# Linear attention and a GELU MLP in one kernel: a written-out order for the first group's attention, and idle matmuls between the first transposes

## The chip, the cores and the metric

The kernel runs on one core of a Trainium2 chip. The metric is the device time of one execution in microseconds (us), lower is better. TensorE (PE) multiplies matrices, VectorE (DVE), ScalarE (ACT) and GpSimd (POOL) work elementwise, SyncE (SP) issues transfers; GpSimd issues transfers too, and each such issue takes its time.

## The reference

Linear attention with a decay per head, then a two-layer MLP. Batch 4, 8 heads, 768 positions, head size 64; 3072 tokens of width 512, hidden width 2048. Inputs and output are float32.

```python
for b in range(nb):                       # blocks of 64 positions
    intra = einsum('bhic,bhjc->bhij', qb, kb) * Dmask      # Dmask = lam**(i-j), i >= j
    intra = einsum('bhij,bhjd->bhid', intra, vb)
    inter = einsum('bhid,bhde->bhie', qb * lam_pow, kv_state)
    out[:, :, sl] = intra + inter
    kb_dec = kb * rev_pow                                  # lam**(63-pos)
    kv_state = lam_block * kv_state + einsum('bhsd,bhse->bhde', kb_dec, vb)
x = out.transpose(0, 2, 1, 3).reshape(3072, 512)
h = x @ w_in
y = (0.5 * h * (1 + erf(h / sqrt(2)))) @ w_out
```

## The kernel before

The attention goes by chunks of 128 positions, all heads at once: 24 chunks, six for each batch entry. For a chunk the steps are: load k, q and v (cast to bf16 on the way, issued by GpSimd); k^T and q^T with the decay in them (`transposes` on TensorE, or `dma_transposes` by SyncE, for which GpSimd first makes q_hat); `scores` = k^T q^T, masked into sc_m by VectorE; `decay_k`, k times its decay; `next_state`, which adds k_dec^T v to the state (kv_ps); `outputs`, state times q^T plus v times sc_m, emptied into x_t, the transposed input of the MLP.

The MLP goes by groups of four chunks (512 tokens), six groups. A group has 32 blocks of 4 matmuls: 16 blocks of the first layer (`mm1`: h_ps, then GELU on ScalarE into g_t), and 16 of the second (`mm2`: o_ps, then ScalarE copies to o_sb and SyncE writes it out). In group 0 the second layer goes through outputs 0 and 1 in turn, then 2 and 3 in turn.

The chunks 0 to 3 are the opening (`early`), written out by hand with idle matmuls (`keep_warm`) between. The attention of a later chunk n is put among the MLP's blocks of the group before its own: chunks 4 to 7 in group 0, 8 to 11 in group 1, and so on. A table of fractions (`fs`) sets before which block the four steps of a chunk stand: begin (decay on GpSimd, and the loads of a chunk some steps ahead, `prefetch`), transposes, scores with the next state, and outputs. Chunks 4 to 7 use TensorE's transposes, later ones the transposing DMA.

The program is a manual schedule: each engine executes its instructions in the order in which the code emits them, and waits at each for what it needs. So a load that GpSimd issues can stand behind a decay that waits for data, and the other way round. In the order lists and traces, L65 is a load, L87 and L91 the weights' loads, L167 a decay of k on GpSimd, L178 a transpose, L200 scores, L237 a state, L252 and L262 the two parts of outputs, L268 the copy into x_t, L280 and L292 the MLP's matmuls.

The PSUM banks limit what can be in flight: two for "mh" (h_ps, and k^T in the opening), two for "mo" (the second layer, idle matmuls, and q^T in the opening), two for scores, one "t" (transposes of chunks 4 to 7, and kv_ps), one "o" (outputs of the attention).

Of the kernel before, what the change touches and what calls it, by code (L numbers as in the profile page):

```python
# [8 lines left out]
F32 = mybir.dt.float32  # L9
BF16 = mybir.dt.bfloat16  # L10
# [5 lines left out]
def kernel(  # L16
# [10 lines left out]
    nc = tc.nc  # L27
# [11 lines left out]

    M = 4  # L40
    NG = NCH // M
    assert NG * M == NCH and M < NB

    ctx.enter_context(tc.manual_schedule())

# [17 lines left out]
    def load(n, name):  # L63
        raw[n, name] = qkv_pool.tile([128, H, D], BF16, tag=name, name=f"{name}_t")
        nc.gpsimd.dma_start(raw[n, name], chunk_of(name, n))  # L65
# [82 lines left out]
    def bank(shape, dtype, tag, name):  # L148
        return ps.tile(shape, dtype, tag=tag, name=name, bufs=2 if tag in ("sc", "mh", "mo") else 1)
# [7 lines left out]
    def decay_k(c, eng):  # L157

        if c.sb == NB - 1:
            return  # L160
        c.k_dec = work_pool.tile([128, H, D], BF16, tag="kd", name="k_dec")
        if eng is nc.scalar:
            for h in range(H):
                nc.scalar.activation(c.k_dec[:, h, :], c.k[:, h, :], ACT.Copy, scale=lam_k[:, h:h + 1])
        else:
            scale = lam_k if c.early else lam_m
            eng.tensor_mul(c.k_dec, c.k, scale[:, :, None].to_broadcast((128, H, D)))  # L167

    def transposes(c):
        if c.early:  # L170

            t_ps = [bank([128, HP, C], BF16, tag, "t_ps") for tag in ("mh", "mo")]
        else:
            both = bank([128, 2, HP, C], BF16, "t", "t_ps")
            t_ps = [both[:, 0], both[:, 1]]
        for dst, src in zip(t_ps, (c.k, c.q)):
            for hp in range(HP):
                nc.tensor.transpose(dst[:, hp, :], src[:, 2 * hp:2 * hp + 2, :], ident)  # L178
        c.kT = work_pool.tile([128, HP, C], BF16, tag="kT", name="kT")
        c.qT = work_pool.tile([128, HP, C], BF16, tag="qT", name="qT")  # L180
        if c.early and c.n % 2:
            nc.scalar.copy(c.kT, t_ps[0])
        else:
            nc.vector.tensor_copy(c.kT, t_ps[0])  # L184
        nc.vector.tensor_mul(c.qT, t_ps[1], lam_q)  # L185
# [20 lines left out]
    def next_state(c):  # L206
        if c.sb == NB - 1:
            return
        if not c.early:
            return next_state_full(c)  # L210
        kv_ps = bank([128, HP, D], F32, "t", "kv_ps")
        for hp in range(HP):
            for hi in range(2):
                h = 2 * hp + hi
                nc.tensor.matmul(kv_ps[hi * D:(hi + 1) * D, hp, :], c.k_dec[:, h, :], c.v[:, h, :],
                                 start=True, stop=True)
# [11 lines left out]
        old = work_pool.tile([128, HP, D], F32, tag="old", name="old")  # L228
        for hp in range(HP):
            nc.scalar.activation(old[:, hp, :], new[:, hp, :], ACT.Copy, scale=lam_c[:, hp:hp + 1])  # L230
        states[c.n + 1] = new, old

    def next_state_full(c):

# [10 lines left out]
            nc.vector.tensor_mul(new, tmp, lam_blk)  # L245
        states[c.n + 1] = new, None

    def outputs(c, x_t, off):
        o_ps = bank([128, HP, C], F32, "o", "o_ps")
        if c.sb > 0 and not c.early:  # L250
            for hp in range(HP):
                nc.tensor.matmul(o_ps[:, hp, :], states[c.n][0][:, hp, :], c.qT[:, hp, :],  # L252
                                 start=(hp == 0), stop=False, skip_group_check=True)
        elif c.sb > 0:
            for hp in range(HP):
                for hi in range(2):
                    p = slice(hi * D, (hi + 1) * D)
                    nc.tensor.matmul(o_ps[p, hp, :], states[c.n][0][p, hp, :], c.qT[p, hp, :],
                                     start=(hp == 0), stop=False, skip_group_check=True)
        for hp in range(HP):  # L260
            for hi in range(2):
                nc.tensor.matmul(o_ps[hi * D:(hi + 1) * D, hp, :], c.v[:, 2 * hp + hi, :], c.sc_m[:, hp, hi, :],  # L262
                                 start=(c.sb == 0 and hp == 0), stop=True, skip_group_check=True)
        x_o = x_t[:, :, off * C:(off + 1) * C]
        if c.early:
            nc.scalar.copy(x_o, o_ps)
        else:
            nc.vector.tensor_copy(x_o, o_ps)  # L268


    def mlp_blocks(g):
# [4 lines left out]
        def mm1(kf):  # L276
            def run():
                h_ps = bank([128, T], F32, "mh", "h_ps")
                for ki in range(NK1):
                    nc.tensor.matmul(h_ps, w_in_t[:, ki, kf * 128:(kf + 1) * 128], x_t[:, ki, :],  # L280
                                     start=(ki == 0), stop=(ki == NK1 - 1))
# [61 lines left out]
    make_dmask()  # L343
    nc.scalar.activation(warm, pos, ACT.Gelu)

    def keep_warm(n):

        idle_ps = bank([128, 512], F32, "mo", "idle_ps")
        for _ in range(n):
            nc.tensor.matmul(idle_ps, idle[:, :128], idle, start=True, stop=True)  # L350

    def early(s):
        live[s] = begin(s, early=True)
        transposes(live[s])
        decay_k(live[s], nc.scalar if s < 2 else nc.gpsimd)
# [9 lines left out]
    outputs(live[0], xT[0], 0)  # L365
    scores(live[1])
    load_w_in(0)
    keep_warm(1)
    early(2)
    next_state(live[1])  # L370
    scores(live[2])
    outputs(live[1], xT[0], 1)
    keep_warm(1)
    early(3)
    next_state(live[2])
# [12 lines left out]

    total = NK2 * 4 * M * C + M * NK2 * 512
    todo = []  # L390
    for n in range(M, NCH):
        g, i = n // M - 1, n % M
        if g == 0:
            fs = [0.66 + 0.34 * (i + f) / M for f in (-0.5, 0.0, 0.5, 1.05)]
        else:
            at = 0.04 + 0.25 * i
            fs = [at - (0.15 if n == 2 * M else 0.32), None, at, at + 0.25 if i < M - 1 else 0.965]
        todo += [(round((g + f) * total), -kind, n) for kind, f in enumerate(fs) if f is not None]
    todo.sort()
# [61 lines left out]
```

## Time and profile before

| | |
|---|---|
| median of 9 runs | 223.72 us (223.31 to 226.08) |
| profiled execution | 223.31 us, span 221.5 us |
| PE busy | 207.3 us, 94% of the span |
| DVE, ACT, POOL busy | 77.2, 87.6, 104.9 us |
| DMA | 24.35 MB, mean 110 GB/s |
| chain that ended last | PE 77%, DMA 10%, POOL 9% of the span |

A row of the timeline reads: start in us, duration in us, engine, source line, operation, output tile <- input tiles, shape, count, and in brackets the idle time ahead of it with the releaser. A row of the waits reads: total us, times, longest us. "PEclk" is the clock granted to TensorE, as a share of full speed. The landing of a transfer is counted from its issue.

### The profile page before, as it was taken

The page shows a single profiled execution, that of the slowest core. Times are in us where ns is not written, and L with a number is a line of the kernel's source. Part 1 is how long each engine was busy: PE and PEld are TensorE (multiplying, and loading weights), DVE is VectorE, ACT ScalarE, POOL GpSimd, SP SyncE. Part 2 cuts the span into 40 slices and gives each one's busy share as a digit, 9 for nine tenths or more (in the row PEclk, how much of TensorE's full clock was granted, in tenths as well). Part 3 has the DMA queues.
Part 4 walks back from the last instruction along what each step waited for, and adds up shares of the span by engine and source line. Part 5 has one row for each costly group of instructions (what it writes and reads, how often), then busy time and mean ns, then how long its engine had stood idle before and what let it go on. Part 6 is the DMA issues. An engine that isn't in the chain of part 4 may idle for free.

```text
span 221.5 us, 3569 instructions
## 1 busy us (share of the span) xinstructions
PE 207.3 (94%) x1423; PEld 103.8 (47%) x1447; DVE 77.2 (35%) x128; ACT 87.6 (40%) x168; POOL 104.9 (47%) x120
## 2 busy tenths in 40 slices
PE   7789999499799999999999999999999999999993
PEld 2454444255445454444455444544445544444452
DVE  4795000458841362133264243035235233100000
ACT  6985671110255611265511365412365321467121
POOL 8998333899999999084981535032100000000000
PEclk9999999969999999999999999999999999999999
DMA  6999999999999999969999896013242012100112
GB/s 41 139 155 198 195 207 182 155 202 140 152 214 157 148 79 174 157 115 148 77 113 144 74 157 100 3 47 96 95 94 51 3 47 81 61 0 3 47 49 95
DMA packets 100272, 24.35 MB, mean 110 GB/s; under 512 B 92960, under 2 KB 97312, under 8 KB 100256
## 3 DMA queue, kind: packets, MB, share of 16 engines
q0 software_dynamic: 79104, 13.64, 84.7%
q1 hardware_dynamic: 21152, 10.50, 21.5%
q8 instruction: 11, 0.18, 0.4%
q14 instruction: 5, 0.04, 0.1%
HBM read 27.27 MB, written 6.29 MB: 151 GB/s over the span
## 4 chain that ended last, share of the span: by engine, by line
PE 77%; DMA 10%; POOL 9%; issue 2%; DVE 1%; ACT 0%; POOLq 0%
PE o_ps L292 33%; PE h_ps L280 31%; DMA w_out_t<-in_moe_w_out_dram 8%; PE o_ps L262 3%; PE sc_ps L200 3%; PE kv_ps L237 2%; DMA k_t<-in_k_dram 2%; POOL q_t L65 2%; POOL v_t L65 2%; PE o_ps L252 2%; POOL k_t L65 2%; PE o_ps L307 2%; POOL w_in_t L87 1%; POOL w_out_t L91 1%; POOL k_dec L167 1%
## 5 line engine op out<-in xcount | busy, mean ns | idle before, releaser
L280 PE MATMUL h_ps<-x_t,w_in_t 128*128 128x512 bf16 x374 | 84.5, 379 | 2.3 <-DVE x_t L268 1.6
L292 PE MATMUL o_ps<-w_out_t,g_t 128*128 128x512 bf16 x355 | 82.5, 381 | 1.0 <-issue 0.4
L282 ACT ACTIVATE g_t<-h_ps 128x512 bf16<-128x512 f32 x96 | 57.3, 597 | 35.6 <-PE h_ps L280 35.6
L280 PEld LDWEIGHTS <-w_in_t 128*128 128x128 bf16 x384 | 37.2, 98 | 45.1 <-issue 1.7
L292 PEld LDWEIGHTS <-g_t 128*128 128x128 bf16 x368 | 35.0, 98 | 40.2 <-issue 1.0
L297 ACT COPY o_sb<-o_ps 128x512 f32<-128x512 f32 x23 | 13.5, 586 | 89.5 <-PE o_ps L292 86.6
L268 DVE CAST x_t<-o_ps 128x512 bf16<-128x512 f32 x20 | 13.8, 690 | 72.3 <-PE o_ps L262 67.0
L204 DVE TENSOR_TENSOR sc_m<-sc_ps,dmask 128x512 bf16<-128x512 f32 x48 | 30.8, 684 | 13.0 <-PE sc_ps L200 12.8
L65 POOL DMA_DIRECT2D v_t<-in_v_dram x24 | 21.3, 889 | 8.5 <-PE o_ps L262 4.6
L167 POOL TENSOR_TENSOR k_dec<-k_t,lam_m 128x512 bf16<-128x512 bf16 x16 | 16.8, 1050 | 16.8 <-PE kv_ps L237 10.9
L192 POOL TENSOR_TENSOR q_hat<-q_t,lam_p 128x512 bf16<-128x512 bf16 x16 | 16.9, 1054 | 16.6 <-DMA qT<-q_hat 16.5
L65 POOL DMA_DIRECT2D k_t<-in_k_dram x24 | 22.1, 921 | 3.6 <-DMA w_in_t<-in_moe_w_in_dram 1.7
L65 POOL DMA_DIRECT2D q_t<-in_q_dram x24 | 21.5, 896 | 4.4 <-DMA w_out_t<-in_moe_w_out_dram 3.5
L245 DVE TENSOR_TENSOR state<-tmp,lam_blk 128x512 bf16<-128x512 f32 x13 | 10.5, 810 | 0.4
L200 PE MATMUL sc_ps<-qT,kT 64*128 64x128 bf16 x192 | 9.5, 218 | 0.9 <-DVE qT L185 0.9
L262 PE MATMUL o_ps<-sc_m,v_t 128*64 128x128 bf16 x192 | 10.1, 228 | 0.0
L184 DVE COPY kT<-t_ps 128x512 bf16<-128x512 bf16 x6 | 2.5, 422 | 21.0 <-PE t_ps L178 20.8
L350 PE MATMUL idle_ps<-idle 128*128 128x512 bf16 x26 | 8.6, 446 | 1.2 <-DVE idle L94 1.2
L237 PE MATMUL kv_ps<-v_t,k_dec 128*128 128x128 bf16 x64 | 6.4, 222 | 2.5 <-POOL k_dec L167 2.5
L200 PEld LDWEIGHTS <-kT 64*128 64x128 bf16 x192 | 5.6, 94 | 6.0 <-issue 3.4
L244 DVE TENSOR_TENSOR tmp<-kv_ps,state 128x512 f32<-128x512 f32 x12 | 8.2, 681 | 0.0
L262 PEld LDWEIGHTS <-v_t 128*64 128x64 bf16 x192 | 6.2, 111 | 3.1 <-issue 1.0
(56 smaller groups left out, 82.5 us busy)
## 6 DMA issues: line engine op xcount, KB each, us to landing
out_dram<-o_sb SPq DMA_DIRECT2D x23, 256.0 KB, 2.2
k_t<-in_k_dram POOLq DMA_DIRECT2D x24, 128.0 KB, 5.2
q_t<-in_q_dram POOLq DMA_DIRECT2D x24, 128.0 KB, 5.7
v_t<-in_v_dram POOLq DMA_DIRECT2D x24, 128.0 KB, 5.7
w_in_t<-in_moe_w_in_dram POOLq DMA_DIRECT2D x4, 512.0 KB, 7.9
w_out_t<-in_moe_w_out_dram POOLq DMA_DIRECT2D x4, 512.0 KB, 14.9
kT<-k_t SPq DMA_TRANSPOSE x16, 5.0
qT<-q_hat SPq DMA_TRANSPOSE x16, 4.2
```

Source lines behind the costliest of these rows:

```text
L65: nc.gpsimd.dma_start(raw[n, name], chunk_of(name, n))
L167: eng.tensor_mul(c.k_dec, c.k, scale[:, :, None].to_broadcast((128, H, D)))
L192: nc.gpsimd.tensor_mul(q_hat, c.q, lam_p[:, :, None].to_broadcast((128, H, D)))
L200: nc.tensor.matmul(sc_ps[hi][:, hp, :], c.kT[p, hp, :], c.qT[p, hp, :], start=True, stop=True)
L204: nc.vector.tensor_mul(c.sc_m[:, :, hi, :], sc_ps[hi], dmask_r[:, :, hi, :])
L237: nc.tensor.matmul(kv_ps[:, hp, :], c.k_dec[:, 2 * hp:2 * hp + 2, :], c.v[:, 2 * hp:2 * hp + 2, :], start=True, stop=True)
L262: nc.tensor.matmul(o_ps[hi * D:(hi + 1) * D, hp, :], c.v[:, 2 * hp + hi, :], c.sc_m[:, hp, hi, :], start=(c.sb == 0 and hp == 0), stop=Tru ...
L268: nc.vector.tensor_copy(x_o, o_ps)
L280: nc.tensor.matmul(h_ps, w_in_t[:, ki, kf * 128:(kf + 1) * 128], x_t[:, ki, :], start=(ki == 0), stop=(ki == NK1 - 1))
L282: nc.scalar.activation(g_t[:, kf, :], h_ps, ACT.Gelu)
L292: nc.tensor.matmul(om[io], g_t[:, kf, io * C:(io + 1) * C], w_out_t[:, kf, :], start=(kf == 0), stop=(kf == NK2 - 1))
L297: nc.scalar.copy(o_sb, om[io])
```

## The change

Five things change; nothing that is computed does.

1. Loads of the opening: q and k of chunks 2 and 3 go ahead of v of chunks 1, 2 and 3 (k0 q0 v0 k1 q1 k2 q2 v1 k3 q3 v2 v3).
2. Opening: the idle matmuls (26 before, 22 now) stand at other places, three of them between the transposes of k and q of chunk 0; chunk 1's decay of k goes from ScalarE to VectorE; k^T of chunk 2 goes to ScalarE; emptying o_ps and decaying the states come later on ScalarE; the state of chunk 3 moves from ahead of group 0 to block 1 of it. The first mm1 of group 0 is split into 384 and 128 tokens.
3. GpSimd's order for chunks 4 to 9: the decays of 4, 6 and 7 are put between load issues.
4. Chunks 4 to 7: their TensorE steps are placed by a table of blocks (`group0`) in blocks 22 to 31; k^T and x go through ScalarE and not VectorE; both transposes use the two "mh" banks.
5. From chunk 8 on: the fractions change a little and loads run three chunks ahead and not four. The built PE order from the start of group 1 on is the same as before.

```diff
-    for n in range(M):
-        for name in "kqv":
-            load(n, name)
+    for item in "k0 q0 v0 k1 q1 k2 q2 v1 k3 q3 v2 v3".split():
+        load(int(item[1]), item[0])
...
-        if c.early:
-            t_ps = [bank([128, HP, C], BF16, tag, "t_ps") for tag in ("mh", "mo")]
-        else:
-            both = bank([128, 2, HP, C], BF16, "t", "t_ps")
-            t_ps = [both[:, 0], both[:, 1]]
+        t_ps = [bank([128, HP, C], BF16, tag, "t_ps") for tag in ("mh", "mo" if c.early else "mh")]
...
+            if src is c.k:
+                between()
...
-        if c.early and c.n % 2:
+        if c.n > 0:
             nc.scalar.copy(c.kT, t_ps[0])
...
+    def empty_outputs(c):
+        if c.n < 2 * M:
+            nc.scalar.copy(c.x_o, c.o_ps)
+        else:
+            nc.vector.tensor_copy(c.x_o, c.o_ps)
...
+                parts = [(0, T - C), (T - C, T)] if g == 0 and kf == 0 else [(0, T)]
...
+        if s == 1:
+            decay_k(live[s], nc.vector)
+        transposes(live[s], between)
+        if s != 1:
+            decay_k(live[s], nc.scalar if s == 0 else nc.gpsimd)
 
     keep_warm(9)
-    early(0)
-    keep_warm(4)
+    early(0, lambda: keep_warm(3, new=False))
+    keep_warm(2, new=False)
     scores(live[0])
-    keep_warm(4)
+    keep_warm(2, new=False)
     early(1)
-    keep_warm(2)
...
-    keep_warm(5)
+    keep_warm(4)
     outputs(live[3], xT[0], 3)
+    decay_state(live[2])
     make_lam_blk()
-    next_state(live[3])
-    keep_warm(1)
...
+    for n, name in [(4, "k"), (4, "q"), (4, "v"), (5, "k"), (5, "q"), (5, "v"), (6, "k"), (6, "q")]:
+        load(n, name)
+    begin_decayed(4)
+    for n, name in [(6, "v"), (7, "k"), (7, "q"), (7, "v"), (8, "k")]:
+        load(n, name)
+    live[5] = begin(5)
+    begin_decayed(6)
+    for n, name in [(8, "q"), (8, "v")]:
+        load(n, name)
+    begin_decayed(7)
+    next_load[0] = 9
+    prefetch(9)
...
+    x1 = lambda n: outputs(live[n], xT[1], n - M)
+    group0 = {
+        1: [lambda: next_state(live[3])],
+        22: [lambda: transposes(live[4])],
+        24: [lambda: scores(live[4])],
+        25: [lambda: transposes(live[5]), lambda: next_state(live[4]), lambda: x1(4)],
...
+        30: [lambda: x1(6), lambda: scores(live[7])],
+        31: [lambda: next_state(live[7]), lambda: x1(7)],
+    }
...
-        if g == 0:
-            fs = [0.66 + 0.34 * (i + f) / M for f in (-0.5, 0.0, 0.5, 1.05)]
...
-            prefetch(n + 4)
+            prefetch(n + 3)
```

GpSimd in group 0. Before, from v of chunk 6 on, with the decay of chunk 4 (`k_dec_588`, from `k_t_448`) behind the last load of chunk 7:

```order
L65 DMA v_t_464<-in_v_dram 128x8x64
L65 DMA k_t_466<-in_k_dram 128x8x64
L65 DMA q_t_468<-in_q_dram 128x8x64
L65 DMA v_t_470<-in_v_dram 128x8x64
L167 TENSOR_TENSOR k_dec_588<-k_t_448,lam_m_132 128x512
```

Now, from q of chunk 6 on; `k_dec_437`, `k_dec_449` and `k_dec_455` are the decays of chunks 4, 6 and 7, `k_t_447`, `q_t_451` and `v_t_453` the loads of chunk 8:

```order
L65 DMA q_t_435<-in_q_dram 128x8x64
L167 TENSOR_TENSOR k_dec_437<-k_t_421,lam_m_132 128x512
L65 DMA v_t_439<-in_v_dram 128x8x64
L65 DMA k_t_441<-in_k_dram 128x8x64
L65 DMA q_t_443<-in_q_dram 128x8x64
L65 DMA v_t_445<-in_v_dram 128x8x64
L65 DMA k_t_447<-in_k_dram 128x8x64
L167 TENSOR_TENSOR k_dec_449<-k_t_433,lam_m_132 128x512
L65 DMA q_t_451<-in_q_dram 128x8x64
L65 DMA v_t_453<-in_v_dram 128x8x64
L167 TENSOR_TENSOR k_dec_455<-k_t_441,lam_m_132 128x512
```

Chunk 4's decay now stands four loads earlier, and five loads, those of chunk 7 and k of chunk 8 among them, stand behind it.

TensorE at the end of group 0, around the outputs of chunk 7, before (the eight matmuls of a kind are shown once; L280 is the first matmul of group 1):

```order
L200 MATMUL sc_ps_833<-qT,kT 128x128
...
L237 MATMUL kv_ps<-v_t,k_dec 128x128
...
L292 MATMUL o_ps<-w_out_t,g_t 128x512
...
L252 MATMUL o_ps<-qT,state 128x128
...
L262 MATMUL o_ps<-sc_m,v_t 64x128
...
L280 MATMUL h_ps<-x_t,w_in_t 128x512
```

And now:

```order
L198 MATMUL sc_ps_812<-qT,kT 128x128
...
L300 MATMUL o_ps<-w_out_t,g_t 128x512
...
L238 MATMUL kv_ps<-v_t,k_dec 128x128
...
L253 MATMUL o_ps<-qT,state 128x128
...
L263 MATMUL o_ps<-sc_m,v_t 64x128
...
L300 MATMUL o_ps<-w_out_t,g_t 128x512
...
L288 MATMUL h_ps<-x_t,w_in_t 128x512
```

A block of the second layer now stands between the outputs of chunk 7 and their reader, and one between its scores and its state.

ScalarE in the second half of group 0, before and now (g_t is the GELU, o_sb the MLP's output, kT and x_t those of chunks 4 to 7):

```order
L282 ACTIVATE g_t<-h_ps 128x512 x16
L297 COPY o_sb<-o_ps 128x512 x4
L282 ACTIVATE g_t<-h_ps 128x512 x16
```

```order
L180 COPY kT<-t_ps 128x512
L305 COPY o_sb<-o_ps 128x512 x2
L180 COPY kT<-t_ps 128x512
L271 CAST x_t<-o_ps 128x4x128
L180 COPY kT<-t_ps 128x512
L271 CAST x_t<-o_ps 128x4x128
L180 COPY kT<-t_ps 128x512
L271 CAST x_t<-o_ps 128x4x128
L305 COPY o_sb<-o_ps 128x512
L271 CAST x_t<-o_ps 128x4x128
L305 COPY o_sb<-o_ps 128x512
```

Four copies of k^T and four of x stand on ScalarE that stood on VectorE; the x of chunk 7 stands between the last two o_sb.

More of the change, by code (lines that the diff above doesn't have):

```diff
@@ L41 @@
     NG = NCH // M
-    assert NG * M == NCH and M < NB
+    assert NG * M == NCH and M == 4 and NB == 6
     ctx.enter_context(tc.manual_schedule())
@@ L167, in decay_k, with transposes @@
             eng.tensor_mul(c.k_dec, c.k, scale[:, :, None].to_broadcast((128, H, D)))
-    def transposes(c):
-        if c.early:
-            t_ps = [bank([128, HP, C], BF16, tag, "t_ps") for tag in ("mh", "mo")]
-        else:
-            both = bank([128, 2, HP, C], BF16, "t", "t_ps")
-            t_ps = [both[:, 0], both[:, 1]]
+    def transposes(c, between=lambda: None):
+        t_ps = [bank([128, HP, C], BF16, tag, "t_ps") for tag in ("mh", "mo" if c.early else "mh")]
         for dst, src in zip(t_ps, (c.k, c.q)):
@@ L228, in next_state, with decay_state @@
         old = work_pool.tile([128, HP, D], F32, tag="old", name="old")
+        states[c.n + 1] = new, old
+    def decay_state(c):
+        new, old = states[c.n + 1]
         for hp in range(HP):
             nc.scalar.activation(old[:, hp, :], new[:, hp, :], ACT.Copy, scale=lam_c[:, hp:hp + 1])
-        states[c.n + 1] = new, old
     def next_state_full(c):
@@ L246, in next_state_full, with outputs @@
         states[c.n + 1] = new, None
-    def outputs(c, x_t, off):
+    def outputs(c, x_t, off, evacuate=True):
         o_ps = bank([128, HP, C], F32, "o", "o_ps")
@@ L263, in outputs @@
                                  start=(c.sb == 0 and hp == 0), stop=True, skip_group_check=True)
-        x_o = x_t[:, :, off * C:(off + 1) * C]
-        if c.early:
-            nc.scalar.copy(x_o, o_ps)
+        c.x_o, c.o_ps = x_t[:, :, off * C:(off + 1) * C], o_ps
+        if evacuate:
+            empty_outputs(c)
+    def empty_outputs(c):
+        if c.n < 2 * M:
+            nc.scalar.copy(c.x_o, c.o_ps)
         else:
-            nc.vector.tensor_copy(x_o, o_ps)
+            nc.vector.tensor_copy(c.x_o, c.o_ps)
     def mlp_blocks(g):
@@ L278, in run @@
                 h_ps = bank([128, T], F32, "mh", "h_ps")
-                for ki in range(NK1):
-                    nc.tensor.matmul(h_ps, w_in_t[:, ki, kf * 128:(kf + 1) * 128], x_t[:, ki, :],
-                                     start=(ki == 0), stop=(ki == NK1 - 1))
+                parts = [(0, T - C), (T - C, T)] if g == 0 and kf == 0 else [(0, T)]
+                for lo, hi in parts:
+                    for ki in range(NK1):
+                        nc.tensor.matmul(h_ps[:, lo:hi], w_in_t[:, ki, kf * 128:(kf + 1) * 128], x_t[:, ki, lo:hi],
+                                         start=(ki == 0 and lo == 0), stop=(ki == NK1 - 1), skip_group_check=True)
                 nc.scalar.activation(g_t[:, kf, :], h_ps, ACT.Gelu)
@@ L344, with keep_warm, early @@
     nc.scalar.activation(warm, pos, ACT.Gelu)
-    def keep_warm(n):
-        idle_ps = bank([128, 512], F32, "mo", "idle_ps")
+    idle_ps = {}
+    def keep_warm(n, new=True):
+        if new:
+            idle_ps[0] = bank([128, 512], F32, "mo", "idle_ps")
         for _ in range(n):
-            nc.tensor.matmul(idle_ps, idle[:, :128], idle, start=True, stop=True)
-    def early(s):
+            nc.tensor.matmul(idle_ps[0], idle[:, :128], idle, start=True, stop=True)
+    def early(s, between=lambda: None):
         live[s] = begin(s, early=True)
-        transposes(live[s])
-        decay_k(live[s], nc.scalar if s < 2 else nc.gpsimd)
+        if s == 1:
[3 more added lines that the diff above has]
+            decay_k(live[s], nc.scalar if s == 0 else nc.gpsimd)
     keep_warm(9)
-    early(0)
-    keep_warm(4)
+    early(0, lambda: keep_warm(3, new=False))
+    keep_warm(2, new=False)
     scores(live[0])
-    keep_warm(4)
+    keep_warm(2, new=False)
     early(1)
-    keep_warm(2)
     next_state(live[0])
-    outputs(live[0], xT[0], 0)
+    decay_state(live[0])
+    outputs(live[0], xT[0], 0, evacuate=False)
     scores(live[1])
@@ L369 @@
     early(2)
+    empty_outputs(live[0])
     next_state(live[1])
     scores(live[2])
-    outputs(live[1], xT[0], 1)
+    decay_state(live[1])
+    outputs(live[1], xT[0], 1, evacuate=False)
     keep_warm(1)
     early(3)
+    empty_outputs(live[1])
     next_state(live[2])
@@ L416, in step @@
             outputs(live[n], xT[g + 1], n % M)
-    prefetch(2 * M - 1)
     done = 0
@@ L422 @@
             alloc_x(g + 1)
-        for run, cost in mlp_blocks(g):
+        for i, (run, cost) in enumerate(mlp_blocks(g)):
+            if g == 0:
+                for act in group0.get(i, []):
+                    act()
             while todo and todo[0][0] <= done:
```

19 lines of the change are left out of this document (11 added, 8 removed).

## The prediction

> **What bounds the kernel now.** I read the page first, then TensorE's waits, then its timeline around them.
>
> ```profile
> PE 207.3 (94%) x1423; PEld 103.8 (47%) x1447; DVE 77.2 (35%) x128; ACT 87.6 (40%) x168; POOL 104.9 (47%) x120
> PEclk9999999969999999999999999999999999999999
> ...
> PE kv_ps L237 <- POOL k_dec L167: 2.5, 1, 2.5
> PE h_ps L280 <- DVE x_t L268: 1.6, 1, 1.6
> PE sc_ps L200 <- DVE qT L185: 0.9, 2, 0.6
> ```
>
> TensorE is busy 94% of the span, and its clock is below full in one slice of 40. The waits (us in total, times, longest) are few. The timeline of PE shows that all but the opening's lie between 38 and 61 us, at the end of group 0:
>
> ```profile
> 38.67 0.39 PE L178 MATMUL t_ps<-ident,k_t 128*128 128x128 bf16 x4
> 39.43 0.40 PE L178 MATMUL t_ps<-ident,q_t 128*128 128x128 bf16 x4 [0.37 <-DMA q_t<-in_q_dram]
> 39.66 1.03 PE L292 MATMUL o_ps<-w_out_t,g_t 128*128 128x512 bf16 x4
> 41.06 0.40 PE L200 MATMUL sc_ps<-qT,kT 64*128 64x128 bf16 x8 [0.38 <-DVE qT L185]
> 43.98 0.40 PE L237 MATMUL kv_ps<-v_t,k_dec 128*128 128x128 bf16 x4 [2.51 <-POOL k_dec L167]
> ...
> 60.80 1.89 PE L280 MATMUL h_ps<-x_t,w_in_t 128*128 128x512 bf16 x7 [1.55 <-DVE x_t L268]
> 62.62 0.40 PE L200 MATMUL sc_ps<-qT,kT 64*128 64x128 bf16 x8
> ```
>
> From 60.80 to the end PE never waits for more than an issue gap, and the matmuls from the start of group 1 on are the same in both kernels. So the change is worth what it moves the 60.80, less any wait that it creates behind it. A row of the stretch behind the 2.51 us of idleness tells what the clock did:
>
> ```profile
> core 0: us, PE busy (x) PEld busy (x) DVE busy (x) ACT busy (x) POOL busy (x), PEclk, DMA share, GB/s
> 44.00:48.80 4.80, 4.58 (x32) 2.84 (x34) 3.08 (x5) 0.59 (x1) 4.80 (x6) 0.64 2.18 184
> ```
>
> The granted clock was 0.64, so 4.80 x 0.36 = 1.73 us of full-speed work are missing.
>
> **The change part by part.** *Decays of k between GpSimd's loads.* The wait of 2.51 us is GpSimd's order: chunk 4's decay stands behind all twelve loads of chunks 4 to 7, and those loads wait in turn for older transfers (the releasers in brackets).
>
> ```profile
> 30.12 0.88 POOL L65 DMA_DIRECT2D q_t<-in_q_dram  x1 [1.87 <-DMA w_out_t<-in_moe_w_out_dram]
> ...
> 37.77 0.88 POOL L65 DMA_DIRECT2D q_t<-in_q_dram  x1 [1.64 <-DMA w_out_t<-in_moe_w_out_dram]
> 38.71 0.88 POOL L65 DMA_DIRECT2D v_t<-in_v_dram  x1
> 39.67 0.88 POOL L65 DMA_DIRECT2D k_t<-in_k_dram  x1
> ...
> 42.86 1.06 POOL L167 TENSOR_TENSOR k_dec<-k_t,lam_m 128x512 bf16<-128x512 bf16 x1
> ...
> q_t<-in_q_dram POOLq DMA_DIRECT2D x1, 128.0 KB, 12.1
> ...
> k_t<-in_k_dram POOLq DMA_DIRECT2D x1, 128.0 KB, 7.2
> ...
> q_t<-in_q_dram POOLq DMA_DIRECT2D x1, 128.0 KB, 5.4
> ```
>
> Now it stands behind q of chunk 6 (issued 37.77 to 38.65) and k of chunk 4, which had landed by 38.67, when its transposes ran. So it runs from about 38.7 to 39.75, 3.6 us ahead of its new reader (block 25, about 43.35). -2.51. Queued behind it are v6, k7, q7, v7 and k8, issued some 1.0 us later, then k_dec of 6, q8, v8, k_dec of 7, and chunk 9's loads. The landing rows (us from issue) are q5 (30.12 + 12.1 = 42.2), k7 (39.67 + 7.2 = 46.9) and q8: k7 needed 7 us because six or seven loads stood ahead at about 0.9 us each, so a later issue only shortens its stay in the line. Cost 0; at worst all of the 1.05 us reaches the landings. The need by the new order, counted from 39.66 with 0.97 us for a block of four matmuls, 0.33 for scores, 0.45 for transposes, 0.56 for outputs and 0.33 for a state: chunk 5's transposes at 42.9 (q5 42.2), chunk 7's at about 49.9 (k7 46.9, at worst 48.0). Both are covered, the first by 0.7 us.
>
> *k^T and x emptied by ScalarE, blocks in between.* Scores of chunk 4 come after eight matmuls instead of four, and k^T no longer precedes q^T on VectorE: -0.38. x of chunk 7 is now followed by four o_ps matmuls before group 1 reads it, and goes to ScalarE, while before it stood on VectorE behind tmp and state:
>
> ```profile
> 58.73 0.68 DVE L244 TENSOR_TENSOR tmp<-kv_ps,state 128x512 f32<-128x512 f32 x1
> 59.44 0.70 DVE L245 TENSOR_TENSOR state<-tmp,lam_blk 128x512 bf16<-128x512 f32 x1
> 60.07 0.68 DVE L268 CAST x_t<-o_ps 128x512 bf16<-128x512 f32 x1
> ...
> L266 ACT CAST x_t<-o_ps 128x512 bf16<-128x512 f32 x4 | 2.3, 570 | 0.8 <-PE o_ps L262 0.8
> L182 ACT COPY kT<-t_ps 128x512 bf16<-128x512 bf16 x2 | 1.1, 571 | 0.0
> ```
>
> 0.57 us on ScalarE hide under 0.97 us of matmuls: -1.55. ScalarE's eight new pieces (8 x 0.57 = 4.6 us) fit into a stretch of 15 us in which it does four o_sb copies; VectorE loses them. Cost 0; without that cover a late copy would cost at most its own 0.57 us.
>
> *The clock.* With the idle 2.51 us gone, I take the slow stretch to go too. Its price is at most 1.73; the stretch's 0.22 us without PE work need not be lost twice, so at least 1.5. I take 1.6. The Trainium skill, "TensorE: Matmul & The Clock Gate", section "Part 1: The HAM clock gate", lets the clock fall only after an idle window of about 3.4 us; by it a 2.5 us gap alone would not do it. The trace does not agree, unless idleness before the gap was counted in.
>
> *The opening.* Idle matmuls are redistributed (26 become 22), chunk 1's decay moves to VectorE, states are decayed later, and chunk 3's state goes into block 1. Two rows say what limits the first real matmul, and the third what moves:
>
> ```profile
> 19.40 0.10 PEld L280 LDWEIGHTS <-w_in_t 128*128 128x128 bf16 x1 [0.25 <-DMA w_in_t<-in_moe_w_in_dram]
> 19.68 13.97 PE L280 MATMUL h_ps<-x_t,w_in_t 128*128 128x512 bf16 x63 [0.23 <-ACT x_t L266]
> 18.84 0.29 PE L215 MATMUL kv_ps<-v_t,k_dec 128*64 128x64 bf16 x8
> 14.41 1.04 POOL L167 TENSOR_TENSOR k_dec<-k_t,lam_k 128x512 bf16<-128x512 bf16 x1 [0.49 <-DMA k_t<-in_k_dram]
> ```
>
> x of chunk 3 may be ready some tenths sooner, but w_in lands at 19.4, so at most 0.28 us are won, and 0.29 are paid in block 1. And whatever is won there, q of chunk 4 lands when it lands: the 0.37 us wait at 39.43 takes it back. Net 0. Above: k of chunk 3 is now the ninth load and not the tenth, so the 0.49 us wait before its decay goes, and the weight loads behind it may start up to 0.45 us earlier, and with them q4: a gain of 0 to 0.45; I take 0, since the transfers are busy then anyway. Below: see the second rival.
>
> *Group 1.* Its loads keep their rank, but PE arrives 6 us earlier. The first to be needed is q^T of chunk 8, which takes a load, GpSimd's q_hat and a transposing DMA. Before:
>
> ```profile
> 49.45 1.28 SPq L191 DMA_TRANSPOSE kT<-k_t  x1
> 57.61 1.19 SPq L193 DMA_TRANSPOSE qT<-q_hat  x1
> 60.02 1.84 SPq L191 DMA_TRANSPOSE kT<-k_t  x1
> 62.30 1.24 SPq L193 DMA_TRANSPOSE qT<-q_hat  x1
> ...
> qT<-q_hat SPq DMA_TRANSPOSE x1, 4.2
> kT<-k_t SPq DMA_TRANSPOSE x1, 6.5
> qT<-q_hat SPq DMA_TRANSPOSE x1, 5.0
> ```
>
> Counting GpSimd's new order at 0.88 us for a load and 1.06 for an operation, q8 is issued near 45.35, lands by its 5.4 us before at 50.8, and q_hat of 8 ends near 51.9 and its DMA is issued at 52.0. Landings: 4.2 (issued at 57.61, alone), 6.5 and 5.0 (the pair of chunk 9, issued 2.3 us apart). Chunk 8's pair will be 2.5 us apart, so 5.0 is nearest: 57.0. Group 1 starts at 60.80 - 2.51 - 0.38 - 1.55 - 1.6 = 54.76, and scores of 8 come 1.82 us later (62.62 - 60.80), at 56.6. Price +0.4; the ends are 0 and 1.9 (landing 6.5). q^T of chunk 9, by the same count issued at 59.3, lands near 64.3, and is wanted near 65.
>
> **Sum.** -2.51 - 0.38 - 1.55 - 1.6 + 0.4 = -5.64. The profiled execution took 223.31 (span 221.5 and 1.8 around it), the fastest of nine, 0.41 below their median of 223.72. 223.31 - 5.64 = 217.67; by the median 218.08, forecast 218.1.
>
> **Rivals.** All times are by the median. (1) *Landings take the place of the old waits*: chunk 5's q later by more than 0.7 us, or q^T of 8 and 9 late in turn. For it: GpSimd's lines and two outputs written earlier share the same 16 engines. Against: 0.7 to 3 us of slack in every other place. Price 1.0 to 2.0 more: about 219.6. (2) *The clock falls in the opening*: four idle matmuls fewer, and nothing between the outputs of chunk 3 and w_in at 19.4. Against: the longest gap by my count is 0.9 us, and gaps of 1.18 us did not lower the clock before (1.00 up to 17 us):
>
> ```profile
> 6.63 0.40 PE L178 MATMUL t_ps<-ident,q_t 128*128 128x128 bf16 x4 [1.18 <-DMA q_t<-in_q_dram]
> ...
> 0.00:17.00 17.00, 13.08 (x150) 6.98 (x152) 11.97 (x26) 14.26 (x43) 15.64 (x24) 1.00 1.60 114
> ```
>
> Price: the same 1.73 us, of which the q4 wait gives back 0.37: 218.1 + 1.36, about 219.4. The same page of the Trainium skill, section "Part 4: PE-mode transpose", says that transposes do not count as busy, which speaks for this rival, as transposes fill a larger part of an opening with fewer idle matmuls; in this trace they ran between full-clock matmuls, which doesn't decide it. (3) *The clock falls anyway in group 0*, since the gap was not its cause, as by that page's first rule: the 1.6 are not won: 219.7. (4) *Loads behind GpSimd's waits starve*: from k8 on they are issued behind three decays that wait for landings. If they took as long as q5's 12.1 us, q8 (issued near 45.35) would land at 57.5, its q^T at 58.5 + 5.0 = 63.5, and PE would wait 6.9 us: 218.1 + 6.5 = 224.6, slower. It decides once q8 lands some 6 us later than 50.8. Against: the 12 us arose with eight loads, weights among them, in the line. (5) *Nothing measurable*: group 0 bound by landings throughout, each chunk 1.2 us late: about 223.
>
> **Chances.** The forecast's own case 0.60 (217.0 to 218.8), rival 1 0.18, rival 2 0.09, rival 3 0.06, rival 4 0.03, rival 5 0.04. A measurement of this kernel can tell about 0.5%, 1.1 us, from no change. Faster by more than that are the first four cases, 0.93; same 0.04; slower 0.03. Range: the low end is 218.08 less 0.4 (no wait at chunk 8), 0.45 (earlier weights) and 0.13 (1.73 for 1.6), 217.1, opened to 216.9 for the spread of the runs; the high end takes in rivals 1 to 3 with the worst landing: 220.2.
>
> **What would show it.** Right: k_dec of chunk 4 starts before 39.5, no PE wait for it; PEclk 9 in every slice; the first h_ps of group 1 between 54.4 and 55.5; one short wait of scores of chunk 8 for q^T. Wrong: new waits of t_ps for q_t near 43 or 46; PEclk below 1.00 before 24 us or near 45; waits of sc_ps beyond 1 us in group 1; loads after 45 us that take over 10 us to land.

## The result, and the profile after

The changed kernel takes 217.72 us (median of 10 runs, 216.99 to 219.35); before took 224.46 (median of 32 runs, 222.70 to 226.19). The ratio is 0.9723, 95% interval 0.9696 to 0.9749: 6.2 us faster, 5.6 to 6.8 (the two medians alone are 6.74 us apart; the text uses the ratio). The median of 217.72 lies in the predicted range of 216.9 to 220.2, 0.4 under the 218.1 that was forecast. The two profiled executions took 223.31 and 217.72, 5.59 us apart; the sum of the prediction was 5.64.

TensorE's waits after (us in total, times, longest), page rows first:

```profile
PE 204.9 (95%) x1422; PEld 102.7 (48%) x1446; DVE 72.6 (34%) x120; ACT 91.1 (42%) x169; POOL 105.4 (49%) x120
PEclk9999999999999999999999999999999999999999
...
PE sc_ps L198 <- DVE qT L183: 1.1, 3, 0.6
PE t_ps L174 <- DMA q_t<-in_q_dram: 1.1, 2, 0.6
PE h_ps L288 <- DMA w_in_t<-in_moe_w_in_dram: 1.1, 1, 1.1
PE o_ps L259 <- ACT x_t L271: 0.7, 1, 0.7
PE sc_ps L198 <- DMA qT<-q_hat: 0.6, 1, 0.6
```

The three waits of group 0 (2.51 for k_dec, 1.55 for x_t, 0.38 for q^T) and the clock's dip are gone. One wait is new behind group 0, for q^T of chunk 8. TensorE's timeline after, at the places that were shown of before:

```profile
19.89 1.05 PE L288 MATMUL h_ps<-x_t,w_in_t 128*128 128x384 bf16 x8 [1.05 <-DMA w_in_t<-in_moe_w_in_dram]
...
39.65 0.40 PE L174 MATMUL t_ps<-ident,q_t 128*128 128x128 bf16 x4
39.89 1.89 PE L300 MATMUL o_ps<-w_out_t,g_t 128*128 128x512 bf16 x8
41.71 0.40 PE L198 MATMUL sc_ps<-qT,kT 64*128 64x128 bf16 x8
...
43.36 0.39 PE L238 MATMUL kv_ps<-v_t,k_dec 128*128 128x128 bf16 x4
...
53.88 0.81 PE L300 MATMUL o_ps<-w_out_t,g_t 128*128 128x512 bf16 x3 [0.16 <-issue]
54.53 1.89 PE L288 MATMUL h_ps<-x_t,w_in_t 128*128 128x512 bf16 x8
57.05 0.40 PE L198 MATMUL sc_ps<-qT,kT 64*128 64x128 bf16 x8 [0.63 <-DMA qT<-q_hat]
```

From the end of chunk 4's q transposes to the first matmul of group 1 it took 60.80 - 39.66 = 21.14 us before, and 54.53 - 39.89 = 14.64 now. Of the 6.50 won, 0.63 are given back at 57.05. The other engines at the places that matter (GpSimd, ScalarE, SyncE, and the clock of the stretch that was slow):

```profile
38.85 1.06 POOL L167 TENSOR_TENSOR k_dec<-k_t,lam_m 128x512 bf16<-128x512 bf16 x1
51.11 1.04 POOL L190 TENSOR_TENSOR q_hat<-q_t,lam_p 128x512 bf16<-128x512 bf16 x1 [0.28 <-DMA q_t<-in_q_dram]
58.40 1.09 POOL L190 TENSOR_TENSOR q_hat<-q_t,lam_p 128x512 bf16<-128x512 bf16 x1
...
53.77 0.59 ACT L271 CAST x_t<-o_ps 128x512 bf16<-128x512 f32 x1 [0.21 <-PE o_ps L263]
...
52.18 1.19 SPq L191 DMA_TRANSPOSE qT<-q_hat  x1
...
44.00:48.80 4.80, 4.75 (x56) 2.70 (x58) 3.73 (x6) 1.47 (x3) 4.73 (x6) 1.00 1.95 209
```

Chunk 4's decay runs at 38.85, 4.0 us earlier than before (42.86); it ends at 39.91, 3.4 us before its reader kv_ps starts (43.36), which follows the matmuls ahead of it without a gap. x of chunk 7 is ready at 54.36, under the last four o_ps matmuls. The clock of the stretch is 1.00 and not 0.64.

### The profile page after: what moved, and what is told of

Its sections match the earlier page's. It is cut to its first block, busy times and chain, and to the rows that moved or that the text cites. A ratio compares the mean times of both kernels' runs of the same rounds, so it can differ in the third digit from the quotient of the medians.

```text
span 215.9 us, 3545 instructions
## 1 busy us (share of the span) xinstructions
PE 204.9 (95%) x1422; PEld 102.7 (48%) x1446; DVE 72.6 (34%) x120; ACT 91.1 (42%) x169; POOL 105.4 (49%) x120
## 4 chain that ended last, share of the span: by engine, by line
PE 83%; POOL 8%; DMA 6%; issue 1%; ACT 0%; POOLq 0%
PE h_ps L288 38%; PE o_ps L300 34%; DMA w_in_t<-in_moe_w_in_dram 4%; PE o_ps L263 3%; PE sc_ps L198 3%; POOL q_t L65 2%; DMA qT<-q_hat 2%; POOL k_t L65 2%; PE kv_ps L238 2%; POOL v_t L65 2%; PE o_ps L315 2%; PE o_ps L253 2%; POOL k_dec L167 1%; PE t_ps L174 0%; POOL q_hat L190 0%
## 5 line engine op out<-in xcount | busy, mean ns | idle before, releaser
L288 PE MATMUL h_ps<-x_t,w_in_t 128*128 128x512 bf16 (+2 forms) x378 | 84.8, 377 | 1.6 <-DMA w_in_t<-in_moe_w_in_dram 1.1
L273 DVE CAST x_t<-o_ps 128x512 bf16<-128x512 f32 x16 | 11.1, 692 | 73.3 <-PE o_ps L263 73.3
L167 POOL TENSOR_TENSOR k_dec<-k_t,lam_m 128x512 bf16<-128x512 bf16 x16 | 17.3, 1079 | 14.2 <-PE kv_ps L238 8.2
L183 DVE TENSOR_TENSOR qT<-t_ps,lam_q 128x512 bf16<-128x512 bf16 x8 | 5.5, 690 | 18.7 <-PE t_ps L174 18.5
L246 DVE TENSOR_TENSOR state<-tmp,lam_blk 128x512 bf16<-128x512 f32 x13 | 9.8, 756 | 0.5
L361 PE MATMUL idle_ps<-idle 128*128 128x512 bf16 x21 | 7.6, 477 | 1.2 <-DVE idle L94 1.2
L180 ACT COPY kT<-t_ps 128x512 bf16<-128x512 bf16 x7 | 4.1, 580 | 9.4 <-PE t_ps L174 9.4
```

Of the source, the lines that this page charges most:

```text
L273: nc.vector.tensor_copy(c.x_o, c.o_ps)
L288: nc.tensor.matmul(h_ps[:, lo:hi], w_in_t[:, ki, kf * 128:(kf + 1) * 128], x_t[:, ki, lo:hi], start=(ki == 0 and lo == 0), stop=(ki == NK1 ...
```

## Experiments

Twelve kernels, each timed against before. Times below are ratios to before with their 95% intervals; 1% is 2.24 us. The theory: a late k_dec, its slow clock and x on VectorE cost group 0 some 6 us, and GpSimd's line of loads decides how much of a gain survives group 1.

**The two halves apart.** The opening of the changed kernel, with group 0 and all later work as before (the diff is against the changed kernel):

```diff
...
-        if c.n > 0:
+        if c.early and c.n > 0:
             nc.scalar.copy(c.kT, t_ps[0])
...
-        if c.n < 2 * M:
+        if c.early:
             nc.scalar.copy(c.x_o, c.o_ps)
...
-    for n in range(2 * M, NCH):
+    for n in range(M, NCH):
         g, i = n // M - 1, n % M
+        if g == 0:
+            fs = [0.66 + 0.34 * (i + f) / M for f in (-0.5, 0.0, 0.5, 1.05)]
...
-            if g == 0:
-                for act in group0.get(i, []):
-                    act()
+            if g == 0 and i == 1:
+                next_state(live[3])
...
```

> The opening of the changed kernel (order of the first loads, idle matmuls, chunk 1's decay on VectorE, later emptying, chunk 3's state in block 1) with group 0 and all later work as before. Theory (q of chunk 4 lands when it lands, and w_in sets the first real matmul): 0, within -0.3 to +0.5 us of before; the first h_ps at 19.9, no PE wait for q_t of chunk 4, the 2.5 us wait for k_dec still there. Rival (the opening pays by itself): 0.8 us or more faster than before.

Ratio 0.9977 (0.9952 to 1.0002): 0.5 us faster, 0 to 1.1. The first h_ps starts at 19.55 in its profile, chunk 4 waits for no q, and the k_dec wait is there with 2.3 us. It fits neither end well: the opening is worth between nothing and 1 us.

The other half, the opening of before with all the rest changed:

```diff
-    for item in "k0 q0 v0 k1 q1 k2 q2 v1 k3 q3 v2 v3".split():
-        load(int(item[1]), item[0])
+    for n in range(M):
+        for name in "kqv":
+            load(n, name)
...
-    early(0, lambda: keep_warm(3, new=False))
-    keep_warm(2, new=False)
+    early(0)
+    keep_warm(4)
...
-        1: [lambda: next_state(live[3])],
```

> The opening as before, with the changed kernel's group 0 (decays between load issues, blocks 22 to 31, k^T and x of chunks 4 to 7 on ScalarE) and its later loads. Theory (all of the gain is group 0): 5.3 to 6.0 us faster than before, as the whole change; the first h_ps of group 1 near 54.5, PEclk 1.00 from 40 to 50 us. Rival (the opening has a share): at most 4.8 us faster.

Ratio 0.9761 (0.9728 to 0.9793): 5.4 us faster, 4.6 to 6.1. Group 0, with the later loads that belong to it, is the gain. The rest to the whole change (0.9723) agrees with the opening's half microsecond, but the intervals overlap. From chunk 4's q to group 1 its profile has 56.01 - 41.36 = 14.65 us, as the whole change.

**One move alone.** Before, with only chunk 4's decay put behind q of chunk 6:

```diff
...
-    prefetch(2 * M - 1)
+    prefetch(M + 1)
+    load(M + 2, "k")
+    load(M + 2, "q")
+    live[M] = begin(M)
+    decay_k(live[M], nc.gpsimd)
+    load(M + 2, "v")
+    next_load[0] = M + 3
+    prefetch(2 * M - 1)
```

> Before, with one thing moved: chunk 4's decay on GpSimd stands behind the load of q of chunk 6 and not behind v of chunk 7. Theory (the wait costs itself and the slow clock behind it): no PE wait for k_dec, PEclk 1.00 from 44 to 49 us, the 1.55 us wait for x_t and the 0.4 for q^T still there; 3.5 to 4.4 us faster than before. Rival A (the clock falls for another reason): clock still near 0.64 in that stretch, 2.5 us faster. Rival B (landings take the wait's place): new waits of t_ps for q_t of chunks 5 or 6, 1.5 us faster or less.

Ratio 0.9998 (0.9958 to 1.0038): nothing, although the wait is gone and the clock is 1.00 from 44 to 49 us. Both rivals are wrong too. Its timeline of PE, at chunk 5's transposes and at group 1:

```profile
43.99 0.38 PE L178 MATMUL t_ps<-ident,k_t 128*128 128x128 bf16 x4 [0.77 <-DVE tmp L244]
...
58.48 1.89 PE L280 MATMUL h_ps<-x_t,w_in_t 128*128 128x512 bf16 x8 [1.88 <-DVE x_t L268]
62.59 0.40 PE L200 MATMUL sc_ps<-qT,kT 64*128 64x128 bf16 x8 [2.22 <-DMA qT<-q_hat]
```

The gain was already smaller in group 0: chunk 5's transposes now wait 0.77 us until VectorE has read kv_ps, which shares their bank "t". (The changed kernel, whose transposes use the "mh" banks, has no such wait.) Group 1 starts 2.3 us earlier than before, and scores of chunk 8 start at 62.59, where they started at 62.62. The gain turned into a wait for q^T of chunk 8: its q_hat stands on GpSimd behind loads up to chunk 11, and its transfer was issued at 57.29, against 57.61 before. So I took three loads out of that line:

```diff
-            prefetch(n + 4)
+            prefetch(n + 3)
```

> As kdec_early (chunk 4's decay behind q of chunk 6, nothing else of the change), but with loads three chunks ahead and not four, so that three loads less stand ahead of q_hat of chunk 8 on GpSimd. Theory (what kdec_early gained by the wait and the clock it lost in waiting for q^T of chunk 8): q^T of 8 is issued near 54.6 and not 57.3, its wait of 2.2 us goes, 1.8 to 2.7 us faster than before. Rival (group 0's data bound the rest): still as before, within 0.6 us.

Ratio 0.9856 (0.9817 to 0.9894): 3.2 us faster, 2.4 to 4.1. SyncE and PE:

```profile
54.51 1.19 SPq L193 DMA_TRANSPOSE qT<-q_hat  x1
...
57.83 1.89 PE L280 MATMUL h_ps<-x_t,w_in_t 128*128 128x512 bf16 x8 [1.54 <-DVE x_t L268]
60.21 7.07 PE L280 MATMUL h_ps<-x_t,w_in_t 128*128 128x512 bf16 x32
```

q^T of 8 is issued 2.8 us earlier, and no wait stands between 57.83 and 60.21. This is more than the 1.8 to 2.7 expected. From chunk 4's q to group 1 it takes 57.83 - 39.92 = 17.91 us, 3.23 less than before: the 2.51 of the wait and 1.48 of the clock (measured below), less the 0.77 of the new wait. Two moves on GpSimd make about half of the change's gain, and the first is worth nothing without the second (the second without the first was not run).

**What the clock cost.** Before, with idle matmuls in the time of the k_dec wait, which itself stays:

```diff
             scores(live[n])
+            if n == M:
+                fill_ps = bank([128, 512], F32, "mh", "fill_ps")
+                for _ in range(11):
+                    nc.tensor.matmul(fill_ps, idle[:, :128], idle, start=True, stop=True)
             next_state(live[n])
```

> Before, with eleven idle matmuls (11 x 0.216 = 2.4 us at full clock) ahead of chunk 4's state, in the time in which PE waits for k_dec; no result depends on them. The wait itself stays. Theory (idleness lowers the clock): PEclk 1.00 from 44 to 49 us, first h_ps of group 1 about 1.5 us earlier, 1.2 to 1.8 us faster than before. Rival (a 2.5 us gap does not lower the clock, as by the rule of an idle window of about 3.4 us): 0, within 0.4 us of before.

Ratio 1.0000 (0.9972 to 1.0027): no gain, as the rival said, but not for its reason. Two stretches (the granted clock is the third number from the end) and two rows of its PE:

```profile
44.00:48.80 4.80, 4.80 (x45) 2.50 (x43) 3.60 (x7) 0.59 (x1) 4.80 (x7) 1.00 2.16 185
59.40:63.00 3.60, 3.57 (x14) 1.24 (x15) 0.00 (x0) 0.75 (x2) 3.59 (x5) 0.53 1.59 224
...
56.99 0.41 PE L262 MATMUL o_ps<-sc_m,v_t 128*64 128x128 bf16 x8
59.43 3.38 PE L280 MATMUL h_ps<-x_t,w_in_t 128*128 128x512 bf16 x8 [2.02 <-DVE x_t L268]
```

The dip at 44 is gone in this profile: from chunk 4's state to the outputs of chunk 7 it takes 56.99 - 43.62 = 13.37 us, against 58.83 - 43.98 = 14.85 before. That is the price of the slow clock: 1.48 us. But the wait for x of chunk 7, now 2.02 us, brought a fall of its own, and eight matmuls of group 1 took 3.38 us instead of 1.89. So the second wait was filled too:

```diff
+                if g == 1 and kf == 0:
+                    fill_ps = bank([128, 512], F32, "mh", "fill_ps")
+                    for _ in range(8):
+                        nc.tensor.matmul(fill_ps, idle[:, :128], idle, start=True, stop=True)
                 h_ps = bank([128, T], F32, "mh", "h_ps")
```

> As idle_fill, with eight more idle matmuls ahead of the first matmul of group 1, in the time in which PE waits for x of chunk 7 (2.0 us in idle_fill, behind which the clock was low). Nothing else differs from before. Theory (each of the two waits can lower the clock, and the 1.4 us won by the first filling were lost by the second fall): PEclk 1.00 throughout, first h_ps of group 1 near 59.4, then at most 0.6 us of waiting for q^T of chunk 8: 0.6 to 1.4 us faster than before. Rival (group 1 is bound by q^T of chunk 8 near 62.5 whatever the clock does): within 0.4 us of before.

Ratio 0.9953 (0.9926 to 0.9979): 1.1 us faster, 0.5 to 1.7. In its profile the clock is 1.00 from 24 to 66 us. Work that computes nothing, put into two waits, pays a microsecond.

The clock does not fall in every execution. One fall, as in the profile of before, takes 0.008 off the mean clock of an execution. Of the 53 executions of before on which these ratios rest, ten have a mean clock of 0.998 or more, so no such fall, and take 223.2 us on average; 31 with 0.990 to 0.992 take 223.9, and twelve with 0.985 or less take 224.7. So a fall goes with some 0.7 to 0.8 us, less than the 1.48 of the stretch; in `idle_fill` the wait for x was 0.47 us longer, which takes a part of it back. And of the ten such executions of `kdec_early`, six have a mean clock of 0.992 or 0.985, although its profile has 1.00: a fall behind its two later waits may be part of why it gains nothing.

**Idle matmuls of the opening.** The changed kernel with only the first nine:

```diff
-    early(0, lambda: keep_warm(3, new=False))
-    keep_warm(2, new=False)
+    early(0)
     scores(live[0])
-    keep_warm(2, new=False)
...
-    keep_warm(1)
...
-    keep_warm(4)
```

> The changed kernel without idle matmuls behind the first nine (13 of 22 taken out); nothing that is read depends on them. Theory (idleness lowers the clock, and the opening is otherwise bound by landings): PEclk below 1.00 somewhere between 8 and 24 us, 1.0 to 1.9 us slower than the changed kernel. Rival (they do nothing, since no gap in the opening is as long as 2 us): PEclk 1.00 throughout, within 0.4 us.

Ratio 0.9788 (0.9760 to 0.9816), so 1.5 us slower than the change. Stretches, and the first mm1:

```profile
8.00:12.00 4.00, 3.69 (x45) 2.60 (x45) 3.21 (x6) 3.28 (x14) 4.00 (x6) 0.54 2.25 143
20.00:24.00 4.00, 3.88 (x26) 2.01 (x26) 1.39 (x5) 2.14 (x6) 1.82 (x3) 0.50 1.24 207
...
20.63 1.89 PE L288 MATMUL h_ps<-x_t,w_in_t 128*128 128x384 bf16 x8
```

In this execution the clock fell at 8 us and was 0.50 up to 24 us, into the dense matmuls: from the first mm1 to the end of chunk 4's q transposes it took 42.63 - 20.63 = 22.00 us, against 39.89 - 19.89 = 20.00 in the change. That the low clock is what costs the 1.5 us is shown for this execution alone: the other four list a mean clock of 1.00 and take the same time, 219.2 to 219.3 us. (The last section tells why a mean of 1.00 leaves this open.) With only the three between the first k and q taken out:

```diff
-    early(0, lambda: keep_warm(3, new=False))
+    early(0)
```

> The changed kernel without the three idle matmuls between the transposes of k and q of chunk 0; the other nineteen stay. Theory (one gap of 1.2 us is too short to lower the clock, as it was before the change): PEclk 1.00, within 0.4 us of the changed kernel. Rival (these three keep the clock up): PEclk 0.50 from about 8 us on, 1.0 us or more slower, as without any idle matmul.

Ratio 0.9728 (0.9690 to 0.9767): the change's own time. The time fits the theory, its clock does not:

```profile
8.00:12.00 4.00, 3.72 (x46) 2.48 (x46) 3.19 (x7) 3.03 (x13) 4.00 (x6) 0.65 2.37 151
```

In this execution the clock did fall, shortly before 8 us, and nothing was lost by it: the first mm1 starts at 19.23 (19.89 in the change) and chunk 4's q transposes at 39.08 (39.65).

**ScalarE's share.** The changed kernel with k^T and x of chunks 4 to 7 on VectorE:

```diff
-        if c.n > 0:
+        if 0 < c.n < M:
             nc.scalar.copy(c.kT, t_ps[0])
...
-        if c.n < 2 * M:
+        if c.n < M:
             nc.scalar.copy(c.x_o, c.o_ps)
```

> The changed kernel with k^T and x of chunks 4 to 7 emptied by VectorE, as before; the placement in blocks stays. Theory (the placement took away most of the wait for x_t, ScalarE the rest): x of chunk 7 stands behind tmp and state on VectorE and ends near 55.2 instead of 54.4, group 1 starts 0.8 to 1.0 us later, but 0.6 of it is taken out of the wait for q^T of chunk 8: 0.2 to 1.0 us slower than the changed kernel. Rival (ScalarE carries the 1.55 us): 1.5 us or more slower, with waits at every chunk.

Ratio 0.9773 (0.9740 to 0.9807): 1.1 us slower than the change, just above the 1.0 that was expected (the intervals overlap slightly). One row:

```profile
57.36 1.89 PE L288 MATMUL h_ps<-x_t,w_in_t 128*128 128x512 bf16 x8 [0.57 <-DVE x_t L273]
```

From chunk 4's q to group 1 it takes 57.36 - 41.40 = 15.96 us, 1.32 more than the change. The placement alone leaves 0.57 of the 1.55 us wait for x.

**The new wait.** The changed kernel with scores of chunk 8 two blocks later:

```diff
-        at = 0.06 + 0.245 * i
+        at = 0.12 if n == 2 * M else 0.06 + 0.245 * i
...
```

> The changed kernel with scores and state of chunk 8 two blocks later in group 1 (block 4), so 1.73 us later on PE; GpSimd's and SyncE's orders are the same. Theory (the 0.63 us wait of sc_ps for q^T of chunk 8 is a wait for a transfer that lands at 56.9 whatever PE does): that wait gone, 0.5 to 0.6 us faster than the changed kernel, no new wait. Rival (the next transfer, q^T of chunk 9, then sets the pace): a wait of sc_ps for q^T of chunk 9 of about the same length, 0.

Ratio 0.9748 (0.9710 to 0.9785): no gain; the rival was right. The wait moved on to chunk 9, with the same length:

```profile
65.12 0.40 PE L198 MATMUL sc_ps<-qT,kT 64*128 64x128 bf16 x8 [0.62 <-DMA qT<-q_hat]
```

So GpSimd's line must be shorter, too:

```diff
-            prefetch(n + 3)
+            prefetch(n + 2)
```

> As late8, and from chunk 8 on GpSimd loads two chunks ahead instead of three, so that three loads less (2.7 us) stand ahead of q_hat of chunk 9. Theory (GpSimd's line sets when q^T of chunks 8 and 9 land): q^T of 9 is issued near 56.9 instead of 59.5 and lands near 62, no wait of sc_ps for a q^T at all, 0.5 to 0.7 us faster than the changed kernel. Rival (another landing, q of chunk 10 with the shorter lead, takes the wait's place): the same time as the changed kernel, within 0.3 us.

Ratio 0.9704 (0.9657 to 0.9750). No wait for a q^T is left in its profile, and from the start of group 1 to the end it takes 216.3 - 55.57 = 160.7 us, against 215.9 - 54.53 = 161.4 in the change: the 0.6 us of the wait.

```profile
55.57 3.62 PE L288 MATMUL h_ps<-x_t,w_in_t 128*128 128x512 bf16 x16
```

Timed, it can't be told from the change (0.9723, 0.9696 to 0.9749). It is the best version that I have, by the trace and not by the times.

A larger attempt loaded the first quarter of w_in in two halves as well, and put chunk 4 one block later:

```diff
-    load_w_in(0)
+    for lo in (0, 256):
+        nc.gpsimd.dma_start(w_in_t[:, :, lo:lo + 256], w_in_r[:, :, lo:lo + 256])
...
-        22: [lambda: transposes(live[4])],
+        23: [lambda: transposes(live[4])],
...
```

> The changed kernel with scores of chunk 8 two blocks later, the first quarter of w_in loaded in two halves, and chunk 4's transposes one block later (23), scores of 4 and 5, x of 4 moved to fit (blocks 25 to 27). Theory (the first real matmul waits for the landing of the first piece of w_in, and chunk 4 for its q): first h_ps 0.5 to 0.9 us earlier than 19.9, no wait for q_t of chunk 4 over 0.3 us, and with the wait at chunk 8 gone 0.9 to 1.5 us faster than the changed kernel. Rival (landings of chunks 5 to 7 or the VectorE chain bound group 0): group 1 starts no earlier than 54.5, 0.6 us faster or less.

Ratio 0.9868 (0.9826 to 0.9909), 3 us slower than the change, where 0.9 to 1.5 faster was expected. Its PE, and GpSimd at chunk 7's decay and chunk 8's q_hat:

```profile
19.21 1.12 PE L288 MATMUL h_ps<-x_t,w_in_t 128*128 128x384 bf16 x8
...
54.41 3.62 PE L288 MATMUL h_ps<-x_t,w_in_t 128*128 128x512 bf16 x16
...
68.14 0.40 PE L198 MATMUL sc_ps<-qT,kT 64*128 64x128 bf16 x8 [3.71 <-DMA qT<-q_hat]
...
48.35 1.04 POOL L167 TENSOR_TENSOR k_dec<-k_t,lam_m 128x512 bf16<-128x512 bf16 x1 [0.77 <-PE o_ps L263]
52.85 1.04 POOL L190 TENSOR_TENSOR q_hat<-q_t,lam_p 128x512 bf16<-128x512 bf16 x1 [0.83 <-PE o_ps L300]
```

The first matmul came 0.7 us earlier, group 1 only 0.1, and q_hat of chunk 9 at 60.64 and not 58.40, so that q^T of 9 was 3.7 us late. GpSimd's line was 0.5 us behind at q of chunk 6 (issued at 38.46, and at 37.96 in the change), and lost 0.77 and 0.83 us in two waits. The view names TensorE for them, but k of chunk 7 and q of chunk 8 landed 6.9 and 7.0 us from their issue, at 48.2 and 52.8, just ahead of the two operations (6.2 and 5.7 us in the change). Why these landings were slower is open, as is why the transfer of q^T of 9 then took 6.1 us, against 5.5 in `late8`.

## Why the prediction was right, point by point

- *k_dec, 2.51.* Gone, as forecast, at the time forecast (38.85 for 38.7). What the prediction did not see is that this term is worth nothing by itself: `kdec_early` won it, with the clock behind it, and lost most of it again: 0.77 us to a new wait for VectorE, 0.33 to a longer wait for x, and 2.22 to one for q^T of chunk 8. It counted in the sum only because the same change shortened GpSimd's line, which the prediction had priced apart, under group 1.
- *q^T 0.38 and x 1.55.* Gone. `x_on_dve` splits the second: the blocks in between bring 1.0 of it, ScalarE the last 0.57, and some 0.7 more elsewhere in group 0, where the prediction had taken VectorE's relief as 0.
- *The clock, 1.6.* The mechanism is shown by `idle_fill`, which removes the dip without removing the wait: 1.48 us. The forecast took the fall as certain; ten of 53 executions of before have none. Rival 3 is refuted: without the gap the stretch has a clock of 1.00.
- *Group 0 in all.* 6.04 forecast, 6.50 measured. The waits of 4.44 and the clock's 1.48 make 5.92. The rest of 0.58 is open: it is in no wait (the 0.22 us issue gap of before lies inside the stretch that gave the 1.48), and the changed order has no fewer changes between kinds of matmuls.
- *The opening, 0.* The step "w_in lands at 19.4" failed by 0.4: it was issued at 12.0 in both and landed 7.8 us later instead of 7.4, so that PE waited 1.05 us and group 0 was 0.23 later. The pieces of w_in behind it were issued 0.63 us earlier; whether they took its bandwidth was not tried. A difference of 0.4 in one pair of profiles is within what this start varies: in five profiles with the changed opening it lies between 19.55 and 20.39. Both halves timed leave the opening 0 to 1 us of gain.
- *Chunk 8, +0.4.* Measured 0.63. q^T was issued at 52.18 (forecast 52.0) and landed 4.7 us later (5.0), at 56.9; PE was there 0.2 us sooner than forecast. `late8` shows that this price is not for chunk 8 alone: whoever comes sooner waits at chunk 9. The profile of `no_between`, where group 1 starts at 53.96, waits 0.39 us for q^T of chunk 8 and 1.88 for that of 9.
- *Sum.* In the profiles 6.50 - 0.63 - 0.23 = 5.64 against the 5.59 between the executions. That the forecast's 5.64 is so near is partly luck: group 0's terms were 0.46 too small, and the opening and chunk 8 together 0.46 too cheap. The timed gain, 6.2, is 0.6 above the sum, about what `opening_only` gives to the opening that the forecast took as 0.
- *Rival 1* happened on a small scale (0.63 within the forecast's own ends of 0 and 1.9), at the place named. *Rival 2* did not, but it was nearer than the argument said: the kernel without the thirteen idle matmuls takes 1.5 us more, and the 1.00 of the row that the prediction set against it says less than it seems (last section). *Rival 4* did not happen: q of chunk 8 landed 5.7 us from its issue (5.4 forecast), not 12. *Rival 5* is refuted by the 6.2 us.

## What to carry to other kernels

A wait that is removed is worth only what the next one leaves: look on the in-order engine behind it for the transfer that will be wanted next, and move both. Where an engine issues loads and also computes, the lead of its loads is a cost: three loads ahead of an operation are 2.7 us of delay to whoever needs that operation. Idle time of TensorE is dearer than it looks when the clock falls behind it (1.48 us of slower work behind a wait of 2.51 here), and idle matmuls in an unavoidable wait can be worth more than nothing.

## What the hardware showed that I had not expected

The clock fell behind gaps of 2.51 us (before) and 2.02 us (`idle_fill`), and did not fall in the profile of `kdec_early`, where PE waited 1.88 us and 2.22 us within 4.1 us. In `no_between` it was down to 0.50 from 8 to 10 us, behind gaps of no more than 1.24 us. And the same kernel, before, has executions with and without a fall. So no length of a gap decides it in these runs. The Trainium skill, "TensorE: Matmul & The Clock Gate", section "Part 1: The HAM clock gate", says that activity is judged in a free-running window of about 3.4 us; a window whose position is chance would let the same gap fall on either side, but its rule that only a whole idle window lowers the clock does not hold here, with 2.02 us.

The opening varies from one execution to the next by more than the differences sought: in six profiles with before's opening the first matmul of group 0 started at 19.67, 19.68, 19.68, 20.80, 21.03 and 21.40, and chunk 4's q transposes between 39.13 and 41.13. The latest of them (`idle_fill2`) waited 1.72 us for w_in. In the two others (`kdec_early`, `group0_only`) TensorE itself was slow up to 10 us. The idle matmuls behind the first q transposes, in `kdec_early` and in before:

```profile
7.19 1.91 PE L350 MATMUL idle_ps<-idle 128*128 128x512 bf16 x4
...
6.86 1.03 PE L350 MATMUL idle_ps<-idle 128*128 128x512 bf16 x4
```

PEclk reads 1.00 in both. It reads 1.00 in the first 4 us of before as well, where nine idle matmuls take 3.52 us, 0.39 each, against 0.24 for the eight matmuls of 1.89 us above. So in the opening the durations of matmuls tell the clock, and a PEclk or a mean clock of 1.00 does not show that TensorE ran at full speed from the start. None of the five profiles with the changed opening has such slow matmuls behind 7 us; that the three idle matmuls between the first transposes bring this is not shown.

Single profiles are therefore compared from chunk 4 on, and not by their spans.
